# Attention and gated feed-forward on one core: the second half's probabilities split in SBUF and turned by transposing DMAs

## The chip, the cores and the metric

The kernel runs on one core of a Trainium2 chip. The metric is the device time of one launch in microseconds, the median of the runs of one kernel. A profile of one further execution gives the trace from which all rows below are taken. PE is TensorE (PEld its weight loads), DVE is VectorE, ACT ScalarE, POOL GpSimd, SP SyncE; SPq, ACTq and POOLq are the sequencers of the last three, which issue DMAs.

## The reference

Multi-head attention with a learned relative bias, followed by a gated feed-forward layer without a non-linearity. B = 4 batches, H = 8 heads, S = 576 positions, D = 64 per head; d_model = 512, d_ff = 1536.

```python
scores = (q @ k.T) / sqrt(D) + bias[h]      # 576 x 576 for each batch and head
attn = exp(scores - rowmax); attn /= sum(attn) + 1e-9
x = concat_heads(attn @ v)                  # 2304 tokens x 512
out = ((x @ w_a) * (x @ w_b)) @ w_out
```

The bias is a small two-layer function of the relative distance, computed once at the start. All inputs and outputs are 32-bit floats.

## The kernel before

A unit is one batch, one pair of heads and one half of the query positions: `UNITS` lists 16 units with the first 256 queries (c = 0), then 16 with the remaining 320 (c = 1). A unit is cut into query tiles of 128 rows: A0, B0, A1, B1 for c = 0 (A and B are the two heads) and A2, B2, A3, B3, T for c = 1, where T holds the last 64 queries of both heads. There are 64 tiles in the first half and 80 in the second.

`attn_steps` (L615) walks over the tiles with a software pipeline. In step n it loads the bias rows of tile n + 2 through SyncE's queue, and `soft1` (L489) adds the bias to the scores in PSUM and takes the row minimum on VectorE (L496) and the exponential with its row sum on ScalarE (L501). Then come the score products of tile n + 1 (`qk`, L468), the turning of tile n - 2 (`turn`, L538), the value products of the unit whose last tile was n - 3 (`pv`, L581), and `soft2` (L525) of tile n - 1, which makes the reciprocal of the row sum (L529 on GpSimd, L530 on VectorE) and scales the tile in place on GpSimd (L532).

The value products need the probabilities with the key positions on the partitions. `turn` does this with five 128 x 128 products against the identity (L545) into PSUM; the fifth block covers keys 448 to 575 and so overlaps the fourth. ScalarE copies the result to fp16 (L568), and VectorE subtracts that copy from PSUM to make a second fp16 part, which holds the rest of the 32-bit value (L572 for four blocks, L573 for the last 64 keys). In the second half the second part of the last 64 keys is put into the unused half of block 4, so that nine blocks of 128 keys hold both parts. `pv` then runs 14 pairs of products of 320 columns (L594) over the terms of value part and probability part, and the results leave PSUM as two fp16 parts of x, on ScalarE (L606) and VectorE (L608).

Between these steps TensorE's list is filled with pieces of the feed-forward blocks of tokens that are done: products for a and b (L690), then the output products (L739), interleaved by `merge` with counts from `ends`. TensorE's order is the order of the program text. The order on the other engines and on the DMA queues comes from the scheduler, apart from the edges set with `issue_after`: under `late()` an instruction comes behind the last entries of the lists `ttrs`, `exps`, `evs` and `pns` that stand on its own engine; `pns` holds L532. The DMA queue of SyncE carries the bias rows (L445, L448), the keys and queries of a unit (L386, L387) and its values (L205). The bias tile has three buffers, the probability tile `p` three, the turned tile `pt` two, and the PSUM tiles `qk` and `tp` one each. When the second half begins, `chunk_pool(1)` (L659) gives the memory of the first half's `pt` to the second half's tiles, which wait for its last readers.

Of the kernel before, what the change touches and what calls it, by code (L numbers as in the profile page):

```python
# [8 lines left out]
F32 = mybir.dt.float32  # L9
# [19 lines left out]
TOK = 256  # L29
# [5 lines left out]
TILES = []  # L35
# [17 lines left out]
def attention_moe(ctx, tc, q0d, q1d, kd, vd, idn, wp, wa, wb, wo, lsw, lg, rl, out):  # L53
# [398 lines left out]
    def qk(n, pool):  # L452
        u, t = TILES[n]
        ps = pool.tile([128, 2, 512], F32, tag="qk", name="qk", bufs=1)
        q, k = st["qs", u], st["ks", u]
        if u < 2 * NP:
            j = int(t[0] == "B")
            sl, c0 = slice(64 * j, 64 * j + 64), 128 * int(t[1])
            prods = [(q[sl, c0:c0 + 128], k[sl])]
        elif t == "T":  # L460
            prods = [(st["qt", u][:, p, j], k[:, j]) for p in range(2) for j in range(2)]
        else:
            j = int(t[0] == "B")
            c0 = TOK * j + 128 * (int(t[1]) % 2)
            prods = [(q[:, p, c0:c0 + 128], k[:, j]) for p in range(2)]
        for x, (a, b) in enumerate(prods):
            for hf in range(2):
                nc.tensor.matmul(  # L468
                    ps[:, hf, :HB], a, b[:, hf * HB:hf * HB + HB], start=(x == 0), stop=(x == len(prods) - 1)
                )  # L470
        st["qk", n] = ps
# [32 lines left out]
    def pv_first(n, pool):  # L504
# [17 lines left out]
            out=xl, in0=ps[:, :128], scalar=vsc[0][0], in1=xh, op0=ALU.mult, op1=ALU.subtract  # L522
        )

    def soft2(n):  # L525
        u, t = TILES[n]
        p, sm = st.pop(("p", n))
        rc = sm
        nc.gpsimd.tensor_scalar(out=sm, in0=sm, scalar1=1e-9, scalar2=1.0 / (PS if u >= NF else 1.0), op0=ALU.add, op1=ALU.mult)  # L529
        nc.vector.reciprocal(out=rc, in_=sm)  # L530
        pns.append(
            nc.gpsimd.tensor_scalar(out=p, in0=p, scalar1=rc, scalar2=1.0, op0=ALU.mult, op1=ALU.mult)  # L532
        )
        st["pn", n] = p
# [2 lines left out]

    def turn(n, pool):  # L538
        u, t = TILES[n]
        c = UNITS[u][2]  # L540
        p = st.pop(("pn", n))
        tp = pool.tile([128, 5, 128], F32, tag="tp", name="tp", bufs=1)
        for x in range(5):
            c0 = min(128 * x, S - 128)
            nc.tensor.transpose(tp[:, x, :], p[:, c0:c0 + 128], tab["idn"])  # L545
        if u < NP:
            if t[0] == "A":
                st["pt", u] = epool[0].tile([128, 5, 256], F32, tag="pt", name="ptf", bufs=2)
            o = 128 * (t[0] == "B")
            evs.append(nc.scalar.copy(st["pt", u][:, :, o:o + 128], tp))  # L550
            return
        W = 512 + 128 * c
        if u < NF:
            if t == "A0":
                st["pt", u] = cpool[0].tile([128, 5, W], F32, tag="pt", name="ptw", bufs=2)
            o = {"A0": 0, "A1": 128, "B0": 256, "B1": 384}[t]
            nc.scalar.copy(st["pt", u][:, :, o:o + 128], tp)
            return
        if t in ("A0", "A2"):
            st["pt", u] = cpool[0].tile([128, 10 - c, W], F16, tag="pt", name="pt", bufs=2)  # L560
        pt = st["pt", u]
        if t == "T":
            dst = pt.rearrange("p x (h w) -> p x h w", h=2)[:, :, :, 0:64]
            src = tp.rearrange("p x (h w) -> p x h w", h=2)
        else:
            o = {"A0": 0, "A1": 128, "B0": 256, "B1": 384, "A2": 64, "A3": 192, "B2": 384, "B3": 512}[t]
            dst, src = pt[:, :, o:o + 128], tp
        nc.scalar.copy(dst[:, 0:5], src)  # L568
        if not c:
            nc.vector.tensor_tensor(out=dst[:, 5:10], in0=src, in1=dst[:, 0:5], op=ALU.subtract)  # L570
            return
        nc.vector.tensor_tensor(out=dst[:, 5:9], in0=src[:, 0:4], in1=dst[:, 0:4], op=ALU.subtract)  # L572
        nc.vector.tensor_tensor(  # L573
            out=dst[0:64, 4], in0=src[64:128, 4], in1=dst[64:128, 4], op=ALU.subtract
        )

    TERMS = [(0, x, x) for x in range(4)] + [(1, x, x) for x in range(4)]
    TERMS += [(0, x, 5 + x) for x in range(4)] + [(0, 4, 4), (1, 4, 4)]
# [2 lines left out]
    def pv(u, pool):  # L581
        b, hp, c = UNITS[u]
        N = TOK + TAIL * c
        pt = st.pop(("pt", u))
        vs = st["vs", u]
        ps = pool.tile([128, 512], F32, tag="pv", name="pv")
        if u < NF:
            prods = [(vs[:, x], pt[:, x]) for x in range(4)] + [(vs[64:128, 4], pt[64:128, 4])]
        else:
            rows = [slice(64 if vb == 4 and not c else 0, 128) for _, vb, _ in TERMS + LAST[c]]  # L590
            prods = [(vs[sl, part, vb], pt[sl, pb]) for (part, vb, pb), sl in zip(TERMS + LAST[c], rows)]
        for x, (v, p) in enumerate(prods):
            for j in range(2):
                nc.tensor.matmul(  # L594
                    ps[64 * j:64 * j + 64, :N], v[:, j, :], p[:, j * N:j * N + N],
                    start=(x == 0), stop=(x == len(prods) - 1),
                )
        if hp == 0:
            st["x", b, c] = [att.tile([128, KC, TOK], F16, tag=f"x{p}", name=f"x{p}", bufs=2) for p in range(2)]
        xh, xl = st["x", b, c]  # L600
        outs = [(xh[:, hp, :], xl[:, hp, :], ps[:, N - TOK:N], vsc[b][0] if u < NF else 1.0 / PS)]
        if c:
            sl = slice(TAIL * b, TAIL * b + TAIL)
            outs.append((xt[0][:, hp, sl], xt[1][:, hp, sl], ps[:, 0:TAIL], vsc[B + 1][:, b:b + 1]))
        for dh, dl, src, sc in outs:
            nc.scalar.mul(dh, src, sc)  # L606
        for dh, dl, src, sc in outs:
            nc.vector.scalar_tensor_tensor(  # L608
                out=dl, in0=src, scalar=sc, in1=dh, op0=ALU.mult, op1=ALU.subtract
            )  # L610
# [3 lines left out]

    def attn_steps():  # L615
        vgen = [None]
        for n in range(NT + 3):
            u = TILES[n][0] if n < NT else None
            if n == 0:
                qk_pair(0)  # L620
# [32 lines left out]
            if n + 1 < N0 + 2:  # L653
                if n % 2:
                    qk_pair(n + 1)
            elif n + 1 < NT:
                qk(n + 1, qkp)
            if n == B * N0 + 1:
                chunk_pool(1)  # L659
            if n >= 2 and n - 2 < NT:  # L660
                turn(n - 2, tpp)
            if n == N0 + 1:
                pv_first(n - 2, pvp)
            elif n >= 3 and n - 3 < N0:
                if TILES[n - 3][1][0] == "B" and n != N0 + 2:
                    pv_first(n - 3, pvp)
            elif n >= 3 and (n - 2 >= NT or TILES[n - 3][0] != TILES[n - 2][0]):
                pv(TILES[n - 3][0], pvp)
            if 1 <= n <= NT:
                soft2(n - 1)  # L670
# [119 lines left out]
    HALF = 2 * FC + GS  # L790
    LEADS = [3] + [4] * 3 + [8] * 4
    ends = [N0 * (i + 1) + LEADS[i] for i in range(B)] + [B * N0 + N1 * (i + 1) + LEADS[B + i] for i in range(B)]
    ends = [min(NT + 3, x) for x in ends] + [NT + 3]
    asteps = attn_steps()

    def steps(blk):
# [170 lines left out]
```

## Time and profile before

| | |
|---|---|
| median of 3 runs | 794.18 us (793.91 to 796.61) |
| the profiled execution, its own time | 791.7 us |
| its span in the trace | 789.9 us |
| TensorE busy | 756.0 us (96%) |
| VectorE busy | 509.6 us (65%) |
| ScalarE busy | 500.1 us (63%) |
| GpSimd busy | 321.9 us (41%) |

The span is the time from the first to the last instruction in the trace; the execution's own time has 1.8 us around it. Busy time is the union of an engine's instructions, so overlapping matmuls count once. A row of a group of instructions has the number of them, the busy time and the mean duration of one; a row of a timeline has the start, the length, the engine, the line and the tiles that are written and read.

### The profile page before, as it was taken

Reading aid. Unit: us, or ns where it says so; the run is one execution under the profiler, and the core shown is the slowest. Engines: PE = TensorE matmul, PEld = TensorE weight load, DVE = VectorE, ACT = ScalarE, POOL = GpSimd, SP = SyncE. Lnnn points to the kernel's source line nnn. Section 1 sums busy time; section 2 is a strip of 40 time slices with the busy share of each in tenths; the row PEclk is TensorE's granted clock in tenths of the full one; section 3 lists DMA queues with packets and bytes.
Section 4 is the critical chain, followed back from the end, with each engine's and each line's share of the span. In section 5 each row is a group of like instructions: output and inputs, shape, how many; then the busy total and the mean of one; then the engine's idle time right before and its main releaser. Section 6 shows DMA issues by size and latency. Waiting matters only on the chain.

```text
span 789.9 us, 16363 instructions
## 1 busy us (share of the span) xinstructions
PE 756.0 (96%) x5939; PEld 601.1 (76%) x5939; DVE 509.6 (65%) x1203; ACT 500.1 (63%) x1086; POOL 321.9 (41%) x493
## 2 busy tenths in 40 slices
PE   7778899998999999999999999999999999999998
PEld 1245566677876676888888889888988888888886
DVE  7688688589975787658777877777776662110100
ACT  6879787878866787657775776567666663421310
POOL 3448667946742233224443344234433443320200
PEclk9999999999999999999999999999999999999999
DMA  8999575678645545444444443444344211100001
GB/s 258 319 363 320 181 229 177 200 238 266 200 123 171 159 138 154 122 151 124 125 142 144 145 125 109 129 145 125 109 134 141 77 54 54 48 1 27 2 14 40
DMA packets 52979, 114.15 MB, mean 145 GB/s; under 512 B 6564, under 2 KB 10916, under 8 KB 52900
## 3 DMA queue, kind: packets, MB, share of 16 engines
q1 hardware_dynamic: 45744, 97.35, 39.0%
q10 hardware_dynamic: 5876, 10.93, 4.7%
q0 software_dynamic: 1280, 4.84, 1.8%
q8 instruction: 47, 0.77, 0.4%
q14 instruction: 32, 0.26, 0.1%
HBM read 95.91 MB, written 17.18 MB: 143 GB/s over the span
## 4 chain that ended last, share of the span: by engine, by line
PE 72%; DVE 8%; ACT 6%; issue 4%; DMA 4%; POOL 3%; SPq 1%; ACTq 0%; DVEq 0%; POOLq 0%
PE ab L690 27%; PE o L739 19%; PE qk L468 8%; PE tp L545 8%; PE pv L594 6%; PE psta L153 3%; DVE p L496 2%; DMA bias<-bias_d 2%; ACT p L501 1%; DVE wt L270 1%; DMA rv<-vd 1%; DVE w16t L267 1%; POOL wos L312 1%; DMA rvf<-vd 1%; DVE w16t L266 1%
## 5 line engine op out<-in xcount | busy, mean ns | idle before, releaser
L690 PEld LDWEIGHTS <-w16t 128*128 128x128 f16 x2592 | 250.6, 98 | 41.7 <-issue 13.3
L690 PE MATMUL ab<-x,w16t 128*128 128x256 f16 x2304 | 270.1, 273 | 0.4 <-DVE g L700 0.3
L532 POOL TENSOR_SCALAR p<-p,sm 128x576 f32<-128x576 f32 x144 | 125.9, 874 | 65.3 <-DVE sm L530 57.7
L496 DVE CUSTOM_DVE_ANT_0 p<-qk,bias 128x576 f32<-128x576 f32 x144 | 108.3, 754 | 60.9 <-PE tp L545 55.0
L501 ACT ACTIVATE p<-p,mn 128x576 f32<-128x576 f32 x144 | 111.7, 776 | 40.8 <-DVE mn L496 39.8
L739 PE MATMUL o<-wos,gh 128*128 128x512 f32 x384 | 123.2, 402 | 0.0
L715 POOL TENSOR_TENSOR gl<-g,gh 128x256 fp32r<-128x256 f32 x96 | 71.8, 748 | 121.5 <-ACT gh L714 120.1
L529 POOL TENSOR_SCALAR sm<-sm 128x1 f32<-128x1 f32 x144 | 32.1, 223 | 198.4 <-ACT p L501 194.6
L568 ACT CAST pt<-tp 128x640 f16<-128x640 f32 x96 | 66.3, 691 | 70.8 <-PE tp L545 70.2
L545 PE MATMUL tp<-idn,p 128*128 128x128 f32 x720 | 104.5, 276 | 6.8 <-ACT ptf L550 4.2
L545 PEld LDWEIGHTS tp<-idn,p 128*128 128x128 f32 x720 | 83.4, 141 | 20.6 <-issue 8.4
L700 DVE SCALAR_TENSOR_TENSOR g<-ab,wv,asb 128x256 f32<-128x256 f32 x84 | 40.4, 481 | 79.1 <-ACT asb L698 78.3
L739 PEld LDWEIGHTS o<-wos,gh 128*128 128x128 f32 x384 | 68.9, 188 | 16.2 <-issue 3.3
L468 PE MATMUL qk<-ks,qs 128*128 128x288 f32 x384 | 73.0, 312 | 5.2 <-DVE mn L496 5.1
L739 PE MATMUL o<-wos,gl 128*128 128x512 f32 x192 | 75.4, 393 | 0.0
L468 PEld LDWEIGHTS qk<-ks,qs 128*128 128x128 f32 x384 | 56.6, 190 | 14.3 <-DVE mn L496 7.1
L698 ACT ACTIVATE asb<-ab,wv 128x256 f32<-128x256 f32 x84 | 39.3, 468 | 38.3 <-PE ab L690 38.1
L572 DVE TENSOR_TENSOR pt<-tp,pt 128x512 f16<-128x512 f32 x80 | 55.1, 689 | 8.0 <-ACT pt L568 7.9
L714 ACT CAST gh<-g 128x256 fp32r<-128x256 f32 x96 | 38.8, 404 | 33.9 <-DVE g L700 33.7
L530 DVE RECIPROCAL sm<-sm 128x1 f32<-128x1 f32 x144 | 23.3, 162 | 44.1 <-POOL sm L529 43.1
L400 DVE TENSOR_TENSOR ks<-rk,ks 64x576 fp32r<-64x576 f32 x48 | 44.7, 932 | 4.5 <-ACT ks L399 1.7
L739 PEld LDWEIGHTS o<-wos,gl 128*128 128x128 f32 x192 | 36.0, 188 | 8.2
(107 smaller groups left out, 1033.3 us busy)
## 6 DMA issues: line engine op xcount, KB each, us to landing
bias<-bias_d SPq DMA_DIRECT2D x128, 288.0 KB, 2.9
rv<-vd SPq DMA_DIRECT2D x32, 320.0 KB, 3.3
rk<-kd SPq DMA_DIRECT2D x24, 288.0 KB, 3.4
wraw<-wa SPq DMA_DIRECT2D x12, 512.0 KB, 6.9
wraw<-wb SPq DMA_DIRECT2D x12, 512.0 KB, 5.1
wraw<-wo SPq DMA_DIRECT2D x12, 512.0 KB, 4.3
bias_d<-bo ACTq DMA_DIRECT2D x20, 295.5 KB, 3.0
rq<-q1d SPq DMA_DIRECT2D x16, 320.0 KB, 3.8
```

The costliest lines, as they stand in the source:

```text
L400: nc.vector.tensor_tensor(out=ks[ol, j], in0=rk[sl], in1=ks[sl, j].bitcast(F32), op=ALU.subtract)
L468: nc.tensor.matmul(ps[:, hf, :HB], a, b[:, hf * HB:hf * HB + HB], start=(x == 0), stop=(x == len(prods) - 1))
L496: ttr = nc.vector.tensor_tensor_reduce(out=p.rearrange("p (a n) -> p a n", a=2), in0=ps[:, :, :HB], in1=bt.rearrange("p (a n) -> p a n", a=2),
L501: exps.append(nc.scalar.activation(p, p, AF.Exp, bias=mn, scale=-1.0, accum_out=sm))
L532: nc.gpsimd.tensor_scalar(out=p, in0=p, scalar1=rc, scalar2=1.0, op0=ALU.mult, op1=ALU.mult)
L545: nc.tensor.transpose(tp[:, x, :], p[:, c0:c0 + 128], tab["idn"])
L568: nc.scalar.copy(dst[:, 0:5], src)
L572: nc.vector.tensor_tensor(out=dst[:, 5:9], in0=src[:, 0:4], in1=dst[:, 0:4], op=ALU.subtract)
L594: nc.tensor.matmul(ps[64 * j:64 * j + 64, :N], v[:, j, :], p[:, j * N:j * N + N], start=(x == 0), stop=(x == len(prods) - 1),)
L690: nc.tensor.matmul(ab[:, j], w16[nm, f][:, pw, kk, :], xs[px][:, kk, :], start=(x % (3 * KC) == 0), stop=(x % (3 * KC) == 3 * KC - 1),)
L715: nc.gpsimd.tensor_tensor(out=gl, in0=g, in1=gh.bitcast(F32), op=ALU.subtract)
L739: nc.tensor.matmul(o, g[:, sl], wos[f][:, p], start=(f == 0 and x == 0), stop=(f == FC - 1 and x == 2))
```

## The change

For the sixteen units with c = 1 the turning leaves TensorE. `soft2` calls a new function, `split_turn`: GpSimd scales the tile into the first 576 columns of an fp16 tile `ph` (two buffers), VectorE makes the second part of keys 512 to 575 (columns 576 to 639) and of keys 0 to 511 (columns 640 to 1151), and one transposing DMA on SyncE's queue writes the nine blocks of 128 columns, turned, into the unit's `pt`. `pns` now holds VectorE's last instruction of these. The five products, the copy and the two subtractions of `turn` stay for c = 0 alone. The value products of these units are put one tile later in TensorE's list, ahead of that step's other work, and the loop over tiles has one step more. The tiles of a unit lie in another order in `pt` (A2, A3, T, B2, B3), so head A's tail columns follow its main ones and head B's precede them; the results of the two heads are placed so that the main columns agree, and the tail columns leave PSUM by two instructions of 64 rows in place of one of 128.

```diff
+    def split_turn(n, p, rc):
+        u, t = TILES[n]
+        if t == "A2":
+            st["pt", u] = cpool[0].tile([128, 9, 640], F16, tag="pt", name="pt", bufs=2)
+        ph = cpool[0].tile([128, 2 * S], F16, tag="ph", name="ph", bufs=2)
+        nc.gpsimd.tensor_scalar(out=ph[:, :S], in0=p, scalar1=rc, scalar2=1.0, op0=ALU.mult, op1=ALU.mult)
+        for o, c0, c1 in ((S, 512, S), (640, 0, 512)):
+            ins = nc.vector.scalar_tensor_tensor(
+                out=ph[:, o:o + c1 - c0], in0=p[:, c0:c1], scalar=rc, in1=ph[:, c0:c1],
+                op0=ALU.mult, op1=ALU.subtract,
+            )
+        pns.append(ins)
+        o = {"A2": 0, "A3": 128, "T": 256, "B2": 384, "B3": 512}[t]
+        nc.sync.dma_start_transpose(out=st["pt", u][:, :, o:o + 128], in_=ph)
...
         nc.vector.reciprocal(out=rc, in_=sm)
+        if UNITS[u][2]:
+            split_turn(n, p, rc)
+            return
...
-        nc.vector.tensor_tensor(out=dst[:, 5:9], in0=src[:, 0:4], in1=dst[:, 0:4], op=ALU.subtract)
-        nc.vector.tensor_tensor(
-            out=dst[0:64, 4], in0=src[64:128, 4], in1=dst[64:128, 4], op=ALU.subtract
-        )
...
+                o = TAIL * (c - j * c)
                 nc.tensor.matmul(
-                    ps[64 * j:64 * j + 64, :N], v[:, j, :], p[:, j * N:j * N + N],
+                    ps[64 * j:64 * j + 64, o:o + N], v[:, j, :], p[:, j * N:j * N + N],
...
-            outs.append((xt[0][:, hp, sl], xt[1][:, hp, sl], ps[:, 0:TAIL], vsc[B + 1][:, b:b + 1]))
+            for rw, o in ((slice(0, 64), N), (slice(64, 128), 0)):
+                outs.append((xt[0][rw, hp, sl], xt[1][rw, hp, sl], ps[rw, o:o + TAIL], vsc[B + 1][rw, b:b + 1]))
...
-        for n in range(NT + 3):
+        for n in range(NT + 4):
...
+            if n >= B * N0 + 4 and (n - 3 >= NT or TILES[n - 4][0] != TILES[n - 3][0]):
+                pv(TILES[n - 4][0], pvp)
             if n == B * N0 + 1:
                 chunk_pool(1)
-            if n >= 2 and n - 2 < NT:
+            if n >= 2 and n - 2 < B * N0:
                 turn(n - 2, tpp)
...
-            elif n >= 3 and (n - 2 >= NT or TILES[n - 3][0] != TILES[n - 2][0]):
+            elif N0 + 3 <= n < B * N0 + 3 and TILES[n - 3][0] != TILES[n - 2][0]:
                 pv(TILES[n - 3][0], pvp)
...
-    ends = [min(NT + 3, x) for x in ends] + [NT + 3]
+    ends = [min(NT + 4, x) for x in ends] + [NT + 4]
```

## Rows read from the trace of the kernel before

**Rows 1.** The page's first part: busy time of each engine.

```profile
span 789.9 us, 16363 instructions
PE 756.0 (96%) x5939; PEld 601.1 (76%) x5939; DVE 509.6 (65%) x1203; ACT 500.1 (63%) x1086; POOL 321.9 (41%) x493
```

**Rows 2.** Windows: each engine's busy time, granted clock, DMA share, GB/s.

```profile
349.00:629.00 280.00, 278.85 (x2320) 244.38 (x2319) 211.67 (x494) 187.26 (x399) 106.34 (x196) 1.00 0.42 129
629.00:669.00 40.00, 40.00 (x302) 35.10 (x300) 18.80 (x46) 20.56 (x46) 16.89 (x27) 1.00 0.20 58
669.00:790.00 121.00, 117.05 (x832) 99.95 (x830) 13.22 (x28) 28.11 (x63) 20.83 (x29) 1.00 0.06 21
```

**Rows 3.** Waits, 345 to 680: us in total, times, longest.

```profile
POOL sm L529 <- ACT p L501: 120.0, 64, 3.9
...
PEld L594 <- issue: 3.2, 18, 0.4
```

**Rows 4.** The chain that ended last, 340 to 680, by line.

```profile
by line: PE ab L690 36.1%; PE o L739 21.7%; PE qk L468 13.7%; PE tp L545 13.6%; PE pv L594 10.1%; issue 0.9%; DVE p L496 0.8%; DVE vs L432 0.8%; ACT p L501 0.5%; POOL gl L715 0.4%; ACT vs L431 0.4%; ACT pt L568 0.4%; DVE g L700 0.3%; ACT gh
```

**Rows 5.** Tile tp, 349 to 675: ns min/median/max, first and last start.

```profile
L545 PE MATMUL tp<-idn,p x395: 270/273/302, 351.5 to 668.7; 128*128 128x128 f32 x198
L568 ACT CAST pt<-tp x80: 669/692/693, 348.7 to 669.0; 128x640 f16<-128x640 f32 x80
L572 DVE TENSOR_TENSOR pt<-tp,pt x80: 676/691/693, 349.4 to 669.7; 128x512 f16<-128x512 f32 x80
L573 DVE TENSOR_TENSOR pt<-tp,pt x80: 292/293/295, 350.1 to 670.5; 64x128 f16<-64x128 f32 x80
```

**Rows 6.** Timeline of PE, 505 to 524: start, us, engine, line.

```profile
509.50 0.69 PE L468 MATMUL qk<-ks,qs 128*128 128x288 f32 x4
510.03 0.71 PE L545 MATMUL tp<-idn,p 128*128 128x128 f32 x5
510.49 0.70 PE L739 MATMUL o<-wos,gh 128*128 128x512 f32 x2
...
520.31 0.74 PE L545 MATMUL tp<-idn,p 128*128 128x128 f32 x5
520.98 2.09 PE L594 MATMUL pv<-pt,vs 128*64 128x320 f16 x28
```

**Rows 7.** Timeline of DVE and of POOL, same stretch.

```profile
506.93 0.76 DVE L496 CUSTOM_DVE_ANT_0 p<-qk,bias 128x576 f32<-128x576 f32 x1 [2.32 <-PE tp L545]
...
509.31 0.74 POOL L532 TENSOR_SCALAR p<-p,sm 128x576 f32<-128x576 f32 x1 [0.37 <-DVE sm L530]
```

**Rows 8.** Lines 432 and 608: ns min/median/max, first and last start.

```profile
L432 DVE SCALAR_TENSOR_TENSOR vs<-rv,vs,vs x15: 878/1305/1317, 355.5 to 634.8; 128x640 f16<-128x640 f32 x15
...
L608 DVE SCALAR_TENSOR_TENSOR xt<-pv,ts,xt x16: 274/275/277, 369.1 to 674.8; 128x64 f16<-128x64 f32 x16
```

**Rows 9.** DMA, 345 to 680 (the last: whole span): packets, MB, share; us to landing.

```profile
q1 hardware_dynamic: 18676, 36.71, 36.3%
...
bias<-bias_d SPq DMA_DIRECT2D x59, 288.0 KB, 2.8
...
bias_d<-bo POOLq DMA_DIRECT2D x16, 295.5 KB, 6.3
```

**Rows 10.** DMA queue, 676 to 690, when only the fetches of g run.

```profile
q1 hardware_dynamic: 407, 0.37, 8.1%
```

**Rows 11.** Timeline of SP, 340 to 372: issues.

```profile
356.01 0.43 SPq L205 DMA_DIRECT2D rv<-vd  x1
...
370.70 0.33 SPq L448 DMA_DIRECT2D bias<-bias_d  x1
```

**Rows 12.** Waits of SP's queue, 345 to 680.

```profile
SPq L448 <- DVE mn L496: 174.2, 56, 5.2
```

More of the change, by code (lines that the diff above doesn't have):

```diff
@@ L539, in turn @@
         u, t = TILES[n]
-        c = UNITS[u][2]
         p = st.pop(("pn", n))
@@ L551, in turn @@
             return
-        W = 512 + 128 * c
+        o = {"A0": 0, "A1": 128, "B0": 256, "B1": 384}[t]
         if u < NF:
             if t == "A0":
-                st["pt", u] = cpool[0].tile([128, 5, W], F32, tag="pt", name="ptw", bufs=2)
-            o = {"A0": 0, "A1": 128, "B0": 256, "B1": 384}[t]
+                st["pt", u] = cpool[0].tile([128, 5, 512], F32, tag="pt", name="ptw", bufs=2)
             nc.scalar.copy(st["pt", u][:, :, o:o + 128], tp)
             return
[L559 to L571, printed above, removed]
-        nc.vector.tensor_tensor(out=dst[:, 5:9], in0=src[:, 0:4], in1=dst[:, 0:4], op=ALU.subtract)
-        nc.vector.tensor_tensor(
-            out=dst[0:64, 4], in0=src[64:128, 4], in1=dst[64:128, 4], op=ALU.subtract
-        )
+        if t == "A0":
+            st["pt", u] = cpool[0].tile([128, 10, 512], F16, tag="pt", name="pt", bufs=2)
+        dst = st["pt", u][:, :, o:o + 128]
+        nc.scalar.copy(dst[:, 0:5], tp)
+        nc.vector.tensor_tensor(out=dst[:, 5:10], in0=tp, in1=dst[:, 0:5], op=ALU.subtract)
     TERMS = [(0, x, x) for x in range(4)] + [(1, x, x) for x in range(4)]
@@ L600, in pv @@
         xh, xl = st["x", b, c]
-        outs = [(xh[:, hp, :], xl[:, hp, :], ps[:, N - TOK:N], vsc[b][0] if u < NF else 1.0 / PS)]
+        outs = [(xh[:, hp, :], xl[:, hp, :], ps[:, TAIL * c:TAIL * c + TOK], vsc[b][0] if u < NF else 1.0 / PS)]
         if c:
             sl = slice(TAIL * b, TAIL * b + TAIL)
-            outs.append((xt[0][:, hp, sl], xt[1][:, hp, sl], ps[:, 0:TAIL], vsc[B + 1][:, b:b + 1]))
+            for rw, o in ((slice(0, 64), N), (slice(64, 128), 0)):
+                outs.append((xt[0][rw, hp, sl], xt[1][rw, hp, sl], ps[rw, o:o + TAIL], vsc[B + 1][rw, b:b + 1]))
         for dh, dl, src, sc in outs:
```

## The prediction

> **What bounds the kernel now.** I read the engines' shares first [rows 1]: TensorE is busy 756.0 of 789.9 us, nothing else passes 65%. A share over the whole span says little about one stage, so the windows come next [rows 2]. The change touches only the units of the second half, whose 80 query tiles are turned between 351.5 and 668.7 us [rows 5]: (668.7 - 351.5) / 79 = 4.02 us for each tile. In 349 to 629 TensorE is busy 278.85 of 280 us at granted clock 1.00, VectorE 211.67 (76%), ScalarE 187.26, GpSimd 106.34, the DMA engines 0.42. The list of waits says the same from the other side [rows 3]: GpSimd waits 120.0 us for the exponentials, while the longest wait of TensorE is 3.2 us of issue over 18 times. The chain of waits of 340 to 680 [rows 4] is TensorE work in over nine tenths, 13.6% of it turning products (line 545): 46.2 us. So in this stage a tile takes as long as TensorE's hand-written list for it, and work taken out of that list shortens the span until something else needs over 3.45 us a tile.
>
> **What is removed.** Of each tile five turning products. Their durations overlap their neighbours, so I price them by starts [rows 6]: turning starts at 510.03, the next product at 510.49 (0.46 us), and at 520.31 before the value products of 520.98 (0.67 us). At the middle, 0.55 us, 80 tiles make 44 us; the chain's 46.2 us is the check from above. Each tile's 0.69 us copy on ScalarE goes too, and so do VectorE's two subtractions, 0.69 + 0.29 = 0.98 us [rows 5]. Neither engine sets the pace, so these are worth nothing by themselves. The value products keep their number and their width.
>
> **What is added, VectorE.** Two fused operations per tile, 512 and 64 columns, from SBUF. The nearest rows are the 640-column one with the same types, 0.88 us at least, 1.31 us in most cases, and the 64-column one at 0.275 us [rows 8]. Taking off the 128 columns by the 1.0 ns a column between the two subtractions [rows 5], 0.88 becomes 0.75, so the pair costs 1.02 us; from above 1.31 + 0.28 = 1.58 us. VectorE has 211.67 / 70 = 3.02 us a tile now, so 3.06 after (above: 3.62). I take 3.06, because the long 640-column ones start just after GpSimd's operation has begun (509.31 in [rows 7]), and the new ones start only when GpSimd has finished that tile. This lies beside TensorE's 3.45 us, but at 89% of it in place of 76%. The unit's tail columns now leave PSUM in two halves: one more 0.275 us operation per unit, and one on ScalarE, under the same cover. GpSimd's operation keeps its place and its columns at 0.74 us; half-size output could only help.
>
> **What is added, queue and DMA.** No row shows a transposing transfer; it moves 128 x 1152 x 2 B = 288 KB, the size of a bias load. On the DMA engines: the stage's queue spends 36.3% of 335 us x 16 engines on 18676 packets [rows 9], 104 ns for 1966 B each; the fetches of small packets 8.1% of 14 us x 16 on 407 packets of 909 B [rows 10], 45 ns. Time follows bytes, so 1152 pieces of 256 B come to about 0.9 us of all engines; if each piece cost a small packet's 45 ns, 3.2 us. The other transfers need 0.38 x 4.02 = 1.5 us a tile. Sum 2.4 us (below 3.45, hidden), or 4.7 us from above. On SyncE's queue: an issue is 0.33 to 0.43 us [rows 11]; from above, one such for each of nine blocks, 3.9 us. The other issues, one bias load a tile and three loads every five tiles, take about 0.7 us. Sum 1.1 us, or 4.6 us from above. I take the lower values, since one instruction with the bytes of a bias load is nearest to the bias rows.
>
> **What is queued behind it.** The transfer waits at the head of SyncE's queue for VectorE's second part. Behind it stand the bias loads and the next unit's loads. They are no stranger to waiting: a bias load waits 174.2 us over 56 times for the row minimum that frees its buffer [rows 12], lands in 2.8 us [rows 9] and is used three tiles after the buffer came free, some 10 us. A delay of 1 to 3 us is covered.
>
> **When it must land.** The last tile of a unit: its scores are read at 506.93, GpSimd scales it at 509.31 to 510.05 [rows 7], the two parts end about 511.3, and the value products start at 520.98 [rows 6], now one tile (3.5 us) later. At the new pace that leaves about 11 us for issue and landing; a bias load takes 0.4 + 2.8 = 3.2 us, so value products do not wait. The tighter loop is the split tile, of which there are two: GpSimd's 0.74, VectorE's 1.02, some 0.35 of hand-overs, then issue and landing X, before GpSimd may write that buffer again for the second tile after. So a tile cannot take less than (2.1 + X) / 2: 2.65 us at X = 3.2, 3.45 at X = 4.8, and 4.0 at X = 5.9. Below 4.8 nothing is seen; above 5.9 the kernel is slower.
>
> At the entrance, the first new tile's transfer needs memory that the first half's last value products still read, and SyncE waits for them: up to one tile, once. I put 3 us there, and 3 us for VectorE's tighter schedule.
>
> **Sum.** 44 - 3 - 3 = 38 us off the profiled execution's own 791.7: 753.7. The median of the runs shown is 794.18, 2.5 us above that execution, so 756 us is the forecast for the median, with 744 (all 46 us and a little idle time besides) to 768 as its own range.
>
> The Trainium skill (VectorE: DVE Perf Modes, section "The three transpose paths") has 1309 ns for a 128 x 128 turn by DMA against 390 ns on TensorE, and advises TensorE where PSUM will do; this trace disagrees on the second number, since five turns start within 0.46 to 0.67 us. Nine blocks in a row at that DMA figure would be an estimate of 11.8 us, so (2.1 + 11.8) / 2 = 6.95 us a tile and some 1030 us in all. The same skill (DMA: Bandwidth & Descriptors, section "Latency and other measured facts") gives 261 GB/s for a transposing DMA, by which the transfer is 1.13 us and the sum above stands; no run here shows either yet.
>
> **Rivals.**
> *The transposing transfer sets the pace (slower).* Place: SyncE's queue and the two split buffers. For it: nobody has seen its price here, and the loop allows only 4.8 us unharmed. With the nine-fold issue and a bias load's landing X = 3.9 + 2.8 = 6.7, which is 4.4 us a tile: 791.7 + 80 x 0.4 + 2.5 = 826. With 45 ns for each small piece on the DMA engines 4.7 us a tile: 850. With the 6.3 us to landing of the bias stores issued from GpSimd [rows 9] on top of the 3.9 us issue, 6.15 us a tile: 966. It decides from X = 5.9. The Trainium skill's first page above speaks for it. Against it: equal bytes land in 2.8 us. Chance 0.36, mostly between 810 and 900.
> *VectorE takes over (a small gain).* The second part waits for GpSimd's; if nothing fits in between, VectorE idles for 0.37 + 0.74 us a tile. With half of that filled 3.06 + 0.55 = 3.6 us a tile, with the contended price 3.62: 80 x 0.4 = 32 less entrance, or with less filling 15 us: 765 to 785. Against it: ScalarE and GpSimd leave gaps for other work in which VectorE has 1 us a tile to place. Chance 0.13.
> *Nothing to be measured.* X near 5.9, or a VectorE idle for the full 1.1 us (4.17 us a tile): within 0.5% (4 us, about what a measurement of this kernel can tell from no change). Chance 0.05.
> *The forecast*: 0.46.
>
> So faster 0.59, same 0.05, slower 0.36. The range for 8 in 10 runs from 744 to 865: it holds the forecast, the small gain, no change, and the slower case up to X = 7.7; what is left out is the far part of that case.
>
> **What would show it.** Right: no line 545 after 349 us, about 3.5 us from tile to tile, TensorE still busy throughout, VectorE near 88%, transposing transfers landing in under 4.5 us, issue under 1 us. Wrong: TensorE waiting for a transfer before the value products or for GpSimd's split tile, SyncE busy issuing for more than 3 us a tile, or bias loads that land late and VectorE's first operation waiting for them.

## The result, and the profile after

The changed kernel takes 782.43 us (median of 4 runs, 779.96 to 786.78) against 794.04 us (4 runs) of the kernel before: ratio 0.9853, 95% interval 0.9823 to 0.9883. The forecast was 756, so 11.6 us came where 38 were expected. The profiled execution went from 791.7 to 783.58 us.

The page's first part, of the kernel after:

```profile
span 781.7 us, 15679 instructions
PE 724.0 (93%) x5539; PEld 561.1 (72%) x5539; DVE 508.7 (65%) x1219; ACT 454.3 (58%) x1022; POOL 328.4 (42%) x493
```

Windows of the kernel after, columns as in [rows 2] (stretch, busy time of PE, PEld, DVE, ACT, POOL, granted clock, DMA share, GB/s):

```profile
349.00:629.00 280.00, 254.05 (x2010) 212.35 (x2007) 218.26 (x523) 149.84 (x350) 117.58 (x202) 0.98 0.93 209
629.00:669.00 40.00, 39.75 (x298) 33.41 (x296) 16.95 (x44) 15.34 (x39) 14.13 (x24) 1.00 0.47 110
```

TensorE, which had 1.15 us of idle time in 349 to 669 [rows 2], now has 320 - 254.05 - 39.75 = 26.2 us. The granted clock fell from 1.00 to 0.98 in the first window, which is up to 0.02 x 280 = 5.6 us of full speed. So 25 + 5.6 of the 44 us were given back inside the stage. What is left, 13 us, is near the 11.6 of the medians. The profiled execution shows 8: of the other 5 us, 2.3 were lost ahead of the stage, where the change does nothing (its granted clock was 0.91 in 40 to 80 us, against 1.00 before, and the row minimum of the 65th tile, L496, starts at 336.52 us in place of 334.24); the rest is not accounted for, and the 44 and the 5.6 are estimates.

The waits, 340 to 680, of the kernel after (us in total, times, longest):

```profile
POOL sm L544 <- ACT p L501: 90.3, 57, 3.6
ACT p L501 <- DVE mn L496: 79.8, 51, 4.7
POOL ph L530 <- DMA pt<-ph: 50.7, 24, 6.9
DVE ph L532 <- POOL ph L530: 32.0, 42, 2.0
...
PE qk L468 <- DVE mn L496: 26.0, 18, 2.9
PEld qk L468 <- DVE mn L496: 25.1, 18, 3.2
...
DVE x L614 <- ACT x L612: 3.4, 1, 3.4
```

In the waits of before [rows 3] GpSimd waited for ScalarE, and TensorE for no engine by more than 1.9 us in all. Now the score products wait for VectorE's first operation (L496), which must have read the scores of the tile before out of the single PSUM tile: 26.0 us in 18 waits, which is nearly all of TensorE's 26.2 us. ScalarE waits for the same operation. Two waits are new: GpSimd's for a transfer to land before it may write a split tile again, and VectorE's for GpSimd's scaled tile.

The turned tile and its transfer, of the kernel after (the number behind x counts; ns min/median/max, first and last start):

```profile
L538 SPq DMA_TRANSPOSE pt<-ph x80: 1241/1378/2420, 351.2 to 651.7; - x80
...
DMA to landing us min/median/max: 3.2/3.8/5.9
```

The tiles follow each other every (651.7 - 351.2) / 79 = 3.80 us, where [rows 5] gave 4.02 and 3.45 was forecast. The landing counts from the start of the issue, so 3.8 us is what the forecast called X (its 0.4 + 2.8 for a bias load counted the issue twice). TensorE waits 0.2 us in all for a transfer; GpSimd's 50.7 us are the wait that one causes.

VectorE around the end of a unit, a timeline of the kernel after:

```profile
470.42 0.74 DVE L496 CUSTOM_DVE_ANT_0 p<-qk,bias 128x576 f32<-128x576 f32 x1
471.09 0.08 DVE L496 DVE_READ_ACCUMULATOR2_ANT mn<- 128x1 f32 x1
471.09 1.40 DVE L532 SCALAR_TENSOR_TENSOR ph<-p,sm,ph 128x64 f16<-128x64 f32 x2
472.57 0.16 DVE L545 RECIPROCAL sm<-sm 128x1 f32<-128x1 f32 x1
472.95 0.42 DVE L614 SCALAR_TENSOR_TENSOR x<-pv,x 128x256 f16<-128x256 f32 x1 [0.21 <-ACT xt L612]
473.29 0.57 DVE L614 SCALAR_TENSOR_TENSOR xt<-pv,ts,xt 64x64 f16<-64x64 f32 x2
474.04 0.94 DVE L532 SCALAR_TENSOR_TENSOR ph<-p,sm,ph 128x64 f16<-128x64 f32 x2 [0.17 <-POOL ph L530]
474.90 0.88 DVE L432 SCALAR_TENSOR_TENSOR vs<-rv,vs,vs 128x640 f16<-128x640 f32 x1
475.81 0.76 DVE L496 CUSTOM_DVE_ANT_0 p<-qk,bias 128x576 f32<-128x576 f32 x1
```

Between two first operations lie 5.4 us, with two split pairs (1.40 and 0.94 us; a pair is VectorE's two operations of one tile), a unit's results and the next unit's values. Counted over the trace, 19 of the 76 stretches between first operations hold two pairs, 39 hold one and 18 none. TensorE's score products, a timeline of the same kernel:

```profile
471.88 0.77 PE L468 MATMUL qk<-ks,qs 128*128 128x288 f32 x4
472.50 2.79 PE L698 MATMUL ab<-x,w16t 128*128 128x256 f16 x24
476.63 0.79 PE L468 MATMUL qk<-ks,qs 128*128 128x288 f32 x4 [1.34 <-DVE mn L496]
```

The scores of 471.88 are ready at 472.6 and are read only at 475.81, so the next score products start 1.34 us late. And TensorE's tiles do not come evenly; more score products of the same kernel:

```profile
514.53 0.69 PE L468 MATMUL qk<-ks,qs 128*128 128x288 f32 x4
517.79 0.69 PE L468 MATMUL qk<-ks,qs 128*128 128x288 f32 x4
519.79 0.80 PE L468 MATMUL qk<-ks,qs 128*128 128x288 f32 x4
521.67 1.29 PE L468 MATMUL qk<-ks,qt 128*128 128x288 f32 x8
...
533.82 0.78 PE L468 MATMUL qk<-ks,qs 128*128 128x288 f32 x4
...
539.57 0.85 PE L468 MATMUL qk<-ks,qs 128*128 128x288 f32 x2 [2.34 <-DVE mn L496]
```

The first four are 3.26, 2.00 and 1.88 us apart, and TensorE waits for none of them: at this unit's end its list has two tiles within 3.9 us, since its feed-forward pieces are not spread evenly, and the value products come behind. Over the stage 16 of the 76 distances, less TensorE's idle time in them, are under 2.3 us. Only five of the 18 late score products stand at such a place, with 8.4 us of waiting; one is the entrance at 355.21, with 2.9 us; the other twelve, 14.7 us, stand where the list leaves 3.4 to 3.6 us, as at 476.63 and at 539.57 (5.75 - 2.34 = 3.41 us). So it is above all VectorE's list that is uneven: it has 218.26 / 72 = 3.03 us of work a tile on average (72 first operations start in that window), and 4.5 to 7.5 us between two first operations where two pairs stand. Fourteen of the 18 late score products, with 20.8 us, come behind a stretch with two pairs.

### The profile page after: what moved, and what is told of

The parts are those of the page before. It is cut to its first block, busy times and chain, and to the rows that moved or that the text cites. A ratio compares the mean times of both kernels' runs of the same rounds, so it can differ in the third digit from the quotient of the medians.

```text
span 781.7 us, 15679 instructions
## 1 busy us (share of the span) xinstructions
PE 724.0 (93%) x5539; PEld 561.1 (72%) x5539; DVE 508.7 (65%) x1219; ACT 454.3 (58%) x1022; POOL 328.4 (42%) x493
## 4 chain that ended last, share of the span: by engine, by line
PE 44%; DVE 16%; DMA 14%; issue 11%; ACT 7%; POOL 7%; SPq 0%; POOLq 0%; DVEq 0%; ACTq 0%
PE ab L698 16%; PE o L747 13%; DMA pt<-ph 10%; PE qk L468 4%; DVE p L496 4%; PE psta L153 3%; PE pv L599 3%; DVE ph L532 3%; POOL ph L530 3%; DMA bias<-bias_d 3%; ACT p L501 2%; PE tp L562 2%; DVE ks L400 1%; PE pr L828 1%; DVE wt L270 1%
## 5 line engine op out<-in xcount | busy, mean ns | idle before, releaser
L698 PE MATMUL ab<-x,w16t 128*128 128x256 f16 x2304 | 274.4, 275 | 0.6 <-DVE g L708 0.3
L496 DVE CUSTOM_DVE_ANT_0 p<-qk,bias 128x576 f32<-128x576 f32 x144 | 107.9, 751 | 30.7 <-PE tp L562 15.7
L747 PE MATMUL o<-wos,gh 128*128 128x512 f32 x384 | 121.0, 396 | 0.0
L723 POOL TENSOR_TENSOR gl<-g,gh 128x256 fp32r<-128x256 f32 x96 | 74.1, 772 | 93.1 <-ACT gh L722 90.9
L544 POOL TENSOR_SCALAR sm<-sm 128x1 f32<-128x1 f32 x144 | 41.9, 291 | 165.4 <-ACT p L501 161.0
L532 DVE SCALAR_TENSOR_TENSOR ph<-p,sm,ph 128x64 f16<-128x64 f32 (+1 forms) x160 | 85.4, 574 | 32.3 <-POOL ph L530 32.0
L530 POOL TENSOR_SCALAR ph<-p,sm 128x576 f16<-128x576 f32 x80 | 63.4, 793 | 73.5 <-DMA pt<-ph 50.7
L747 PEld LDWEIGHTS o<-wos,gh 128*128 128x128 f32 x384 | 69.5, 188 | 16.2 <-issue 3.1
L550 POOL TENSOR_SCALAR p<-p,sm 128x576 f32<-128x576 f32 x64 | 59.2, 926 | 35.9 <-DVE sm L545 26.6
L562 PE MATMUL tp<-idn,p 128*128 128x128 f32 x320 | 48.4, 283 | 4.8 <-ACT ptf L567 4.5
L562 PEld LDWEIGHTS tp<-idn,p 128*128 128x128 f32 x320 | 37.6, 144 | 15.2 <-issue 5.4
L753 ACT COPY osb<-o 128x512 f32<-128x512 f32 x18 | 10.5, 585 | 57.8 <-PE o L747 42.0
```

The source lines that it names most:

```text
L496: ttr = nc.vector.tensor_tensor_reduce(out=p.rearrange("p (a n) -> p a n", a=2), in0=ps[:, :, :HB], in1=bt.rearrange("p (a n) -> p a n", a=2),
L530: nc.gpsimd.tensor_scalar(out=ph[:, :S], in0=p, scalar1=rc, scalar2=1.0, op0=ALU.mult, op1=ALU.mult)
L532: ins = nc.vector.scalar_tensor_tensor(out=ph[:, o:o + c1 - c0], in0=p[:, c0:c1], scalar=rc, in1=ph[:, c0:c1], op0=ALU.mult, op1=ALU.subtract,
L698: nc.tensor.matmul(ab[:, j], w16[nm, f][:, pw, kk, :], xs[px][:, kk, :], start=(x % (3 * KC) == 0), stop=(x % (3 * KC) == 3 * KC - 1),)
L723: nc.gpsimd.tensor_tensor(out=gl, in0=g, in1=gh.bitcast(F32), op=ALU.subtract)
L747: nc.tensor.matmul(o, g[:, sl], wos[f][:, p], start=(f == 0 and x == 0), stop=(f == FC - 1 and x == 2))
```

## The experiments

Three theories were to be told apart. S: the loop over two split tiles. D: full DMA engines. V: VectorE has too much work at the units' ends. All idle times below are of TensorE in 349 to 669, made as above; ratios are to the kernel before, run on the same chip.

| run | median us | ratio, 95% interval | idle us | GpSimd waits for transfers, us | VectorE waits for the scaled tile, us |
|---|---|---|---|---|---|
| the changed kernel | 782.43 | 0.9853 (0.9823 to 0.9883) | 26.2 | 50.7 | 32.0 |
| e1, three split tiles | 768.71 | 0.9653 (0.9579 to 0.9727) | 16.2 | none | 16.2 |
| e2, five blocks turned | 774.47 | 0.9752 (0.9701 to 0.9803) | 21.2 | 22.2 | 23.0 |
| e3, no 512-column operation | 765.98 | 0.9636 (0.9594 to 0.9678) | 13.9 | 32.7 | 33.5 |
| e4, plain copy | 771.73 | 0.9707 (0.9664 to 0.9751) | 16.0 | 41.0 | 23.8 |
| e5, e1 and e3 together | 761.51 | 0.9582 (0.9542 to 0.9622) | 8.7 | none | 23.0 |
| e6, e1 without bias loads | 768.54 | 0.9692 (0.9644 to 0.9740) | 16.3 | none | 16.8 |
| e7, order, three split tiles | 768.44 | 0.9670 (0.9607 to 0.9733) | 15.3 | 42.9 | 0.7 |
| e8, the old edge, three | 768.84 | 0.9684 (0.9645 to 0.9722) | 17.8 | none | 15.3 |
| e9, queries on GpSimd, three | 776.79 | 0.9802 (0.9741 to 0.9864) | 22.7 | 1.1 | 23.6 |
| e10, keys and queries on GpSimd | 788.06 | 0.9922 (0.9891 to 0.9953) | 28.8 | 6.1 | 37.6 |
| e11, order, four split tiles | 756.42 | 0.9520 (0.9504 to 0.9537) | 8.1 | 0.5 | none |
| e12, before, keys and queries on GpSimd | 793.28 | 0.9996 (0.9975 to 1.0016) | 1.2 | | |
| e13, four split tiles alone | 770.12 | 0.9691 (0.9638 to 0.9744) | 16.2 | none | 16.5 |
| e14, order, two split tiles | 798.52 | 1.0055 (1.0019 to 1.0091) | 38.3 | 138.2 | 16.5 |

**e1: a third split tile.**

```diff
-        ph = cpool[0].tile([128, 2 * S], F16, tag="ph", name="ph", bufs=2)
+        ph = cpool[0].tile([128, 2 * S], F16, tag="ph", name="ph", bufs=3)
```

> The changed kernel with a third buffer for the split tile, nothing else. Theory S (the loop over two split tiles: GpSimd waits 50.7 us for transfers to land, VectorE's second part comes late, the next tile's first VectorE operation queues behind it, and TensorE's score products wait): those waits go, TensorE's 25 us of idle time in 349 to 669 mostly go, about 760 us. Theory D (the DMA engines are full: share 0.85 to 0.99 in that stretch): waits only move, within 3 us of the changed kernel's 782. Theory V (VectorE has too much to do where a unit's preparation meets two split operations): GpSimd's waits go, TensorE's stay, 778 to 782.

GpSimd's wait for transfers is gone and 13.7 us come back (the four runs lie from 764 to 773 us), but 16.2 us of idle time stay. Theory S holds for about half of the loss.

**e2: five of nine blocks turned.**

```diff
-        nc.sync.dma_start_transpose(out=st["pt", u][:, :, o:o + 128], in_=ph)
+        nc.sync.dma_start_transpose(out=st["pt", u][:, 0:5, o:o + 128], in_=ph[:, 0:640])
...
-            prods = [(vs[sl, part, vb], pt[sl, pb]) for (part, vb, pb), sl in zip(TERMS + LAST[c], rows)]
+            prods = [(vs[sl, part, vb], pt[sl, pb - 5 if c and pb > 4 else pb]) for (part, vb, pb), sl in zip(TERMS + LAST[c], rows)]
```

> Only the first five of nine blocks are turned by the DMA (VectorE still makes both parts); the value products read those blocks in place of the other four, so the second part of keys 0 to 511 is left out of the result. Theory D: the transfer costs the DMA engines 1.05 in place of 1.9 us, the share falls to about 0.75, and the time to about 758. Theory S: the landing falls from 3.8 to about 3 us, so part of the waits go, 765 to 772. Theory V: VectorE's work is the same, 778 to 782.

The landing falls to 3.1 us and GpSimd's wait to 22.2 us; 8 us of the time go, a little less than S had for it and far less than D.

**e3: VectorE without the 512-column operation.**

```diff
-        ph = cpool[0].tile([128, 2 * S], F16, tag="ph", name="ph", bufs=2)
+        ph = phs[n % 2]
...
-        for o, c0, c1 in ((S, 512, S), (640, 0, 512)):
+        for o, c0, c1 in ((S, 512, S),):
...
-            xt.extend(cpool[0].tile([128, KC, B * TAIL], F16, name=f"xt{p}") for p in range(2))
+            xt.extend(cpool[0].tile([128, KC, B * TAIL], F16, name=f"xt{p}") for p in range(2)); phs.extend(cpool[0].tile([128, 2 * S], F16, name=f"ph{p}") for p in range(2)); [nc.gpsimd.memset(ph[:, 640:], 0.0) for ph in phs]
```

> All nine blocks are turned, but VectorE's 512-column operation is left out: those columns of two fixed split tiles are zeroed once, so the second part of keys 0 to 511 is left out of the result. Theory V: VectorE loses 0.75 us a tile, TensorE's waits for the row minimum go, about 758. Theory D: the DMA engines carry the same, 778 to 784. Theory S: the loop is shorter by 0.75 us, so part of the waits go, 768 to 775.

16.5 us come back with the DMA share no lower (0.96 in 349 to 629, against 0.93): between what V and S had said. It leaves both waits in place (32.7 and 33.5 us). The operation stands in the loop as well as in VectorE's list, so this run does not tell S from V.

**e4: the same bytes, not turned.**

```diff
-        nc.sync.dma_start_transpose(out=st["pt", u][:, :, o:o + 128], in_=ph)
+        nc.sync.dma_start(out=st["pt", u][:, :, o:o + 128], in_=ph.rearrange("p (x n) -> p x n", n=128))
```

> The same transfer without turning: a plain DMA copies the nine blocks of the split tile to the same places of the turned tile, partition by partition, so the value products use unturned probabilities. It separates the turning from the moving of 288 KB in 256 B pieces. If turning itself is the price (issue of 1.4 us in place of 0.4, and 25 ns a piece): issue 0.4 us, DMA share near 0.7, 760 by theories D and S. If any 1152 pieces of 256 B cost this much: DMA share and time as in the changed kernel, 778 to 784. Theory V: 778 to 782 either way.

The DMA queue, 345 to 680, of the changed kernel and then of e4 (packets, MB, share; for an issue KB where known and us to landing):

```profile
q1 hardware_dynamic: 113536, 60.61, 81.4%
...
pt<-ph SPq DMA_TRANSPOSE x80, 3.8
```

```profile
q1 hardware_dynamic: 112258, 60.60, 68.4%
...
pt<-ph SPq DMA_DIRECT2D x80, 288.0 KB, 3.4
```

Against the 18676 packets and 36.3% of [rows 9], the turned transfers add 94860 packets and 45.1% of 335 us x 16: 25.5 ns a packet, 1.89 us of all engines a tile. The plain ones cost 18.4 ns a packet, 1.34 us a tile. So turning costs 1.4 times moving the same pieces, and even without it 16 us of idle time stay. Neither prediction of D fits, and the 771.7 us are neither the 760 of S nor the 778 of V.

**e5: e1 and e3 together** (three fixed split tiles, no 512-column operation).

> The two that helped most, together: three split tiles, and VectorE's 512-column operation left out (the second part of keys 0 to 511 is zero in the result). If the loop over the split tiles and VectorE's work are the whole cause: TensorE's idle time in 349 to 669 under 5 us and the time 752 to 757, near the 748 that the removed products alone would give. If the DMA engines (share about 1.0 in both) hold the rest: no better than the 766 of the two fixed split tiles, 763 to 767.

The idle time falls to 8.7 us; the profiled execution took 757.7 us, the median of 4 is 761.5. By its idle time it is better than either part (by its time the intervals touch), with the DMA share at 1.01. It misses the 752 to 757, and its median lies under the 763 to 767 that full DMA engines would have made; e6 asks about them alone.

**e6: no bias loads after the first of the second half, three split tiles.**

```diff
...
+        if n > B * N0: st["bias", n] = st["one"]; return
...
-        bt = pool.tile([128, S], F32, tag="bias", name="bias", bufs=bufs)
+        bt = st["one"] = pool.tile([128, S], F32, tag="bias", name="bias", bufs=bufs)
```

> Three split tiles, and no bias loads after the first of the second half: that one bias tile is used for all, so the result has the wrong bias rows there; 288 KB a tile and one issue a tile less. If full DMA engines hold the rest: the share falls to about 0.8, and the time from 769 to about 758. If VectorE's order holds it (its first operation of a tile stands in its list behind a wait for GpSimd and the split operations of the tile before): the DMA share falls and the time stays, 766 to 771.

Windows of e1 and then of e6, 349 to 629:

```profile
349.00:629.00 280.00, 264.07 (x2152) 223.83 (x2151) 229.15 (x549) 159.88 (x371) 128.29 (x214) 0.99 0.95 215
```

```profile
349.00:629.00 280.00, 263.95 (x2164) 224.21 (x2163) 229.09 (x550) 158.34 (x369) 130.58 (x215) 0.99 0.66 136
```

The DMA share falls from 0.95 to 0.66, the transfers land in 3.2 in place of 3.8 us, and the time stays: 768.5 against 768.7 us. Theory D is out as a bound of its own with three split tiles. With two, a shorter landing still shortens the loop, as e2 shows.

**e7: the split operations behind the next first operation, three split tiles.**

```diff
...
+        late_parts.append((n, p, rc, ph))
+
+    def parts(n, p, rc, ph):
+        u, t = TILES[n]
         for o, c0, c1 in ((S, 512, S), (640, 0, 512)):
...
             if n < NT:
                 soft1(n)
+            if n > B * N0 + 1 and late_parts:
+                with tc.issue_after(ttrs[-1].ins):
+                    parts(*late_parts.pop())
```

> Three split tiles, and the split operations of a tile are put behind the first VectorE operation of two tiles later (traced one step later, with an edge), so that VectorE does not wait for GpSimd ahead of it. All work stays. If VectorE's order is what makes the row minimum late: VectorE's waits for GpSimd's scaled tile (16 us with three split tiles) go, TensorE's idle time falls from 16 us to under 6, 756 to 762. If VectorE simply has too much work at the units' ends, or the DMA engines are the cause: 766 to 772.

The pair of a tile now stands behind the first operation of the second tile after it, where the text of the changed kernel has it behind that of the next. By its time alone the order does nothing. The waits say more: VectorE's for the scaled tile fell from 16.2 to 0.7 us, and GpSimd's for transfers came back, from none to 42.9 us, because each split tile is now held for about a tile longer. One wait took the place of the other.

**e8: the old edge.** `pns` holds GpSimd's scaling again, with three split tiles.

```diff
-        nc.gpsimd.tensor_scalar(out=ph[:, :S], in0=p, scalar1=rc, scalar2=1.0, op0=ALU.mult, op1=ALU.mult)
+        ins = nc.gpsimd.tensor_scalar(out=ph[:, :S], in0=p, scalar1=rc, scalar2=1.0, op0=ALU.mult, op1=ALU.mult)
...
-            ins = nc.vector.scalar_tensor_tensor(
+            nc.vector.scalar_tensor_tensor(
```

> Three split tiles, and the list that orders the preparation of keys, queries and values behind the tiles holds GpSimd's scaling again, as before the change, in place of VectorE's second split operation. If that edge is what crowds the preparation into the wait for the scores: 760 to 764. If it is the amount or the waits: 766 to 771.

No difference to e1: with three split tiles the edge plays no part.

**e9 and e10: preparation on GpSimd, three split tiles.**

```diff
-            nc.vector.tensor_tensor(out=ks[ol, j], in0=rk[sl], in1=ks[sl, j].bitcast(F32), op=ALU.subtract)
+            (nc.gpsimd if UNITS[u][2] else nc.vector).tensor_tensor(out=ks[ol, j], in0=rk[sl], in1=ks[sl, j].bitcast(F32), op=ALU.subtract)
...
-            nc.vector.tensor_tensor(out=d[:, 1], in0=s, in1=d[:, 0].bitcast(F32), op=ALU.subtract)
+            (nc.gpsimd if c else nc.vector).tensor_tensor(out=d[:, 1], in0=s, in1=d[:, 0].bitcast(F32), op=ALU.subtract)
```

> Three split tiles, and the two subtractions that prepare a unit's queries (0.69 and 0.28 us on VectorE, sixteen times) are done on GpSimd. All work stays. Theory V (the amount of VectorE's work where a unit's preparation meets the split operations paces TensorE): 1 of about 15.5 us a unit goes from VectorE, the 16 us of idle time with three split tiles fall by some 4 us, 764 to 767. If GpSimd, which starts the split, is itself late by this: 768 to 775.

> As the run before, and the two subtractions of the keys (0.75 us each on VectorE) on GpSimd too: 2.5 us a unit off VectorE, about what the 512-column operations are in three tiles. Theory V: idle time of TensorE near 8 us, 760 to 764. If GpSimd's longer operations then hold back its scaling: 768 to 780.

Both are slower than e1 (only the second line is changed in e9), and both are slower than even the worse case had it: 776.8 against 768 to 775, 788.1 against 768 to 780. Groups of e10 on GpSimd, 349 to 669 (count, busy us, mean ns of one, idle time before):

```profile
L400 POOL TENSOR_TENSOR ks<-rk,ks 64x576 fp32r<-64x576 f32 x30 | 46.5, 1550 | 4.5 <-POOL sm L544 2.7
...
L419 POOL TENSOR_TENSOR qs<-rq,qs 128x512 fp32r<-128x512 f32 x15 | 21.5, 1435 | 1.2
```

A subtraction of 0.75 us takes GpSimd 1.55 us, and it stands in GpSimd's list ahead of a reciprocal's preparation or a scaling. VectorE, with 2.5 us a unit less to do, then waits 37.6 us for scaled tiles in place of 16.2. These runs move work and slow GpSimd at once, so by themselves they do not show that the amount of VectorE's work is free. They show that a late GpSimd costs more than 2.5 us a unit of VectorE's work; theory V, as I had put it, is left to e11.

**e11: the order, with four split tiles** (e7 with `bufs=4`).

> The split operations two tiles behind, with four split tiles in place of three, since with three GpSimd waited 43 us for transfers again. If that wait hid the gain of the order: TensorE's idle time from 15 to under 8 us, 758 to 763. If VectorE's amount of work holds: 766 to 770.

Windows of e11, then its split operations as a group (busy us, mean ns | idle before):

```profile
349.00:629.00 280.00, 272.20 (x2210) 233.23 (x2209) 234.32 (x563) 163.04 (x380) 131.74 (x221) 0.99 1.01 221
629.00:669.00 40.00, 39.75 (x342) 34.44 (x341) 6.22 (x14) 13.68 (x33) 12.91 (x19) 1.00 0.09 31
```

```profile
L536 DVE SCALAR_TENSOR_TENSOR ph<-p,sm,ph 128x512 f16<-128x512 f32 x80 | 61.9, 773 | 0.0
...
L536 DVE SCALAR_TENSOR_TENSOR ph<-p,sm,ph 128x64 f16<-128x64 f32 x80 | 30.3, 379 | 0.0
```

VectorE in e11, its first operations and the split pairs:

```profile
508.91 0.75 DVE L496 CUSTOM_DVE_ANT_0 p<-qk,bias 128x576 f32<-128x576 f32 x1
...
509.59 0.94 DVE L536 SCALAR_TENSOR_TENSOR ph<-p,sm,ph 128x64 f16<-128x64 f32 x2
...
513.15 0.75 DVE L496 CUSTOM_DVE_ANT_0 p<-qk,bias 128x576 f32<-128x576 f32 x1
...
513.82 1.40 DVE L536 SCALAR_TENSOR_TENSOR ph<-p,sm,ph 128x64 f16<-128x64 f32 x2
```

All the work of the changed kernel is done, and the time is 756.42 us, 38 us under the kernel before and 26 under the changed one, better than both and than the 758 to 763 expected. The idle time before the split pair, which was 32.0 us in the changed kernel, is 0.0, and each of the 76 stretches between two first operations holds one pair. The transfers start from 350.1 to 623.9 us, so a tile takes 273.8 / 79 = 3.47 us, where 3.45 was forecast. What idle time is left, 8.1 us, lies before 438 us but for 0.3. VectorE is busier than ever (234.32 of 280 us, 84%), and the DMA share is 1.01; neither hurts. So the amount of VectorE's work is not what cost the time, and theory V falls. What counts is how late its list lets the first operation of the next tile come, waits included. The order takes the waits and the double pairs out together; no run parts the two.

**e12: the control for e10 in the kernel before.**

> The kernel before, with the same four subtractions of the second half's keys and queries on GpSimd and the turning on TensorE. VectorE has 24% idle time there and TensorE none, so by theory V nothing changes: 793 to 796. If taking these operations off VectorE helped for another reason, it would show here too, under 788.

No difference, ratio 0.9996. In the kernel before, neither this work on VectorE nor its longer time on GpSimd reaches TensorE.

**e13 and e14: the buffers without the order, the order without the buffers.**

> The changed kernel with four split tiles and its own order. If the buffers alone bring the forecast time: 755 to 758. If the order is needed (with three split tiles GpSimd already waited for no transfer, so a fourth has nothing to give): as with three, 766 to 771, and TensorE's idle time again about 16 us.

> The changed kernel's two split tiles, with the split operations put behind the first VectorE operation of two tiles later. If the order alone brought it: 756 to 762. If the loop over the split tiles binds (the second part comes a tile later, so each buffer is held for about a tile longer and GpSimd waits for the landing in nearly every tile): slower than the changed kernel, 785 to 815.

Waits of e13 and then of e14, 345 to 670:

```profile
DVE ph L532 <- POOL ph L530: 16.5, 28, 1.1
PE qk L468 <- DVE mn L496: 15.9, 15, 2.9
```

```profile
POOL ph L530 <- DMA pt<-ph: 138.2, 66, 6.9
...
PE qk L468 <- DVE mn L496: 38.1, 27, 3.4
PEld qk L468 <- DVE mn L496: 29.6, 22, 3.5
```

A fourth split tile by itself gives nothing over a third (770.1 against 768.7 us), and the order with two split tiles is 16 us worse than the changed kernel. Only both together bring 756. The order also moves the transfer one tile back and shifts some entries of the other lists; the three runs with the order differ among each other in the number of split tiles alone, as do the three without it.

## Why the prediction was wrong

- **TensorE's list, 44 us: right.** No turning product is left in the second half, and TensorE's busy time, 756.0 us before [rows 1], is 41.9 us lower in e11, in which little waits:

```profile
PE 714.1 (95%) x5539; PEld 558.3 (74%) x5539; DVE 509.5 (68%) x1219; ACT 455.4 (60%) x1022; POOL 331.2 (44%) x493
```

- **VectorE's two operations: right in size.** The group's rows of the kernel after, 349 to 660:

```profile
L532 DVE SCALAR_TENSOR_TENSOR ph<-p,sm,ph 128x512 f16<-128x512 f32 x80 | 59.5, 744 | 0.0
...
L532 DVE SCALAR_TENSOR_TENSOR ph<-p,sm,ph 128x64 f16<-128x64 f32 x80 | 32.3, 404 | 32.3 <-POOL ph L530 32.0
```

  The 512 columns take 744 ns against the 0.75 us of the forecast, the 64 columns 404 ns against 0.275. The forecast took the lower price because the pair starts only when GpSimd has finished that tile. The lower price held for 58 of the 80 tiles. In the other 22 the 64 columns took over 0.35 us, each time beside GpSimd's subtraction for the feed-forward block (L723), and ended 0.08 us after it. So the pair of 471.09 above takes 1.40 us and that of 474.04 only 0.94:

```profile
471.01 0.73 POOL L723 TENSOR_TENSOR gl<-g,gh 128x256 fp32r<-128x256 f32 x1
```

  GpSimd's scaling has its 0.745 us at the median [rows 7: 0.74], so half-size output did not help.
- **The step that failed: "Below 4.8 nothing is seen", and the 3 us for "VectorE's tighter schedule".** Both were made with averages, a tile every 3.45 us. The landing came out at 3.8 us, under the 4.8, and yet GpSimd waited 50.7 us for it and VectorE 32.0 us for GpSimd; in place of the 3 us TensorE waited 26.0 - 2.9 = 23.1 us for VectorE's first operation, and up to 5.6 us of full speed went besides. By the averages both still fit: the loop by the forecast's sum takes (2.1 + 3.8) / 2 = 2.95 us a tile (from GpSimd's start to the landing the trace has 6.3 us on average, 3.15 a tile, and up to 9.5 us), and VectorE has 3.03 us of work. But the scheduler's list for VectorE puts the split pair, with its wait for GpSimd, ahead of the next tile's first operation, on which TensorE's score products hang, and it puts two pairs there in 19 stretches. e1 shows the loop's share (14 us), e11 against e13 that of the order (14 us). They hide each other: removing one wait with too few buffers makes the other (e7, e14). With two split tiles and the order (e14) the loop binds in nearly every tile, 66 waits and 138.2 us.
- **The rival that came.** "VectorE takes over", at 0.13 and 765 to 785 us, named half of the mechanism: the second part waits for GpSimd's, 32.0 / 80 = 0.4 us a tile where it had put 0.55. It was priced as an average too, and without the loop, which makes GpSimd late (16.2 us of that wait stay without it, in e1). That the time fell into its 765 to 785 us is in part luck.
- **The transfer as the pace: wrong as a rival, as forecast.** The issue takes 1.38 us, over three times the value taken and far from the 3.9 of the bound. The DMA engines carry it for 1.89 us a tile, between the bounds of 0.9 and 3.2; with the forecast's 1.5 us for the other transfers that is 3.4 us a tile, beside TensorE's 3.45. e6 and e11 show that this is covered. Bias loads, 3.5 us to landing, make nobody wait, and the value products wait 0.2 us for a transfer.
- **The two numbers of the Trainium skill.** Nine blocks land in 3.8 us, about 0.42 us each, so the 1309 ns that the Trainium skill has for one turn by DMA (VectorE: DVE Perf Modes, section "The three transpose paths") is not a price for each block of a larger transfer here. 294912 B in 1.89 us of all engines are 156 GB/s, below the 261 GB/s of the Trainium skill (DMA: Bandwidth & Descriptors, section "Latency and other measured facts"); the measurement decides.
- **The entrance: right in size by luck.** TensorE idles 2.94 us ahead of the score products at 355.21, once, for VectorE's first operation. The forecast had SyncE waiting for the last readers of the old memory; in this trace its transfers wait for VectorE and GpSimd only. What waits is VectorE, 3.4 us for the results of the first half's last value products (L614 in the waits above), with two split pairs and the next unit's preparation still ahead of the first operation.

Not settled: what part of the clock's 5.6 us is cost of the idle time. The granted clock was 0.66 in 355 to 360 and 0.72 in 370 to 375, each with an idle spell of 2.9 or 2.8 us just before or in it, and 1.00 in 385 to 390, after a spell of 0.8 us. Figures between 0.5 and 1.00 mean that both levels, 1.2 and 2.4 GHz, were granted within the stretch. A grant of 0.91 stands in 40 to 80 of this profile too, far from the change.

## What to carry to other kernels

When work leaves the busiest engine, look up who produces what that engine waits for next, and read that engine's list in the tightest stretch, not its average: here 3.03 us of VectorE work a tile under 3.45 us of TensorE time was still late, since its list had two split pairs ahead of some first operations and none ahead of others, while TensorE's list left 3.4 us there, or 2. A step that waits for another engine belongs behind the operation on which the bound hangs, and a step put later holds its buffer longer, so order and buffer count have to be changed together; either alone moved the wait to the other place. A DMA share near 1 was no bound here: with it at 0.66 the time was the same, and at 1.01 came the best time, with 0.8 us of TensorE's waits for landings in all.

## What the runs showed of the hardware

- A transposing DMA of 128 x 1152 fp16 values from SBUF to SBUF: 1.24 to 2.42 us of SyncE's queue to issue (median 1.38), 3.2 to 5.9 us to landing (median 3.8), 25.5 ns a packet of 256 B against 18.4 ns for plain pieces of the same size (both by difference to the kernel before, with the other transfers beside them).
- Landings stretch under it only a little: bias loads went from 2.8 us [rows 9] to 3.5 us with the DMA share at 0.93.
- GpSimd needs 1.55 and 1.44 us (means in e10) for subtractions that VectorE does in 0.75 and 0.69 us (medians of lines 400 and 419 in the changed kernel).
- VectorE's split pair takes 1.40 in place of 0.94 us where GpSimd's subtraction for the feed-forward block (L723) runs beside its first operation: that one ends 0.08 us after GpSimd's, in 22 of 22 cases, and the excess is all in it. Beside GpSimd's memset or its one-column operation (L414, L544) 19 such operations kept their 0.27 to 0.29 us.
